# A long-convolution gate with a feed-forward branch: two equal column halves become 256 and 384, and the stages are ordered by half

## The chip, the cores and the metric

The kernel runs on one core of one Trainium2 chip. Five engines work side by side, each through its own queue in order: TensorE (PE in the profile, PEld for its weight loads), VectorE (DVE), ScalarE (ACT), GpSimd (POOL) and SyncE (SP). They wait for each other by semaphores. Transfers between the chip's memory (HBM) and the on-chip buffer (SBUF) are issued here by SP and POOL. Matmuls write to PSUM, and ScalarE or VectorE copies from there. The metric is the device time of one launch in microseconds (us).

## What is computed

`S` is 2048 positions, `D` 640 channels, `F` 1728. All inputs are bfloat16.

```python
x  = A_q
xn = _layernorm(x, axis=-1)
# A: short shift convolution, product, long convolution by FFT over 2*S
k_shift = sum(k_pad[:, t:t + S, :] * shift_k[:, ks - 1 - t] for t in range(ks))   # ks = 4
kv = k_shift * v
y  = irfft(rfft(kv padded to 2*S) * rfft(ssm_k padded to 2*S))[:S]
y  = y + kv * ssm_D
s  = xn * y
# B: feed-forward on the same xn
h  = gelu(xn @ w1 + b1)
g  = silu(h @ w2 + b2)
return x + s * g
```

## The kernel before

The Fourier transform over 2048 positions is done by matmuls, as a transform over 128 points and one over 16. Positions lie as 128 partitions by 16 columns of positions (`NT = 16`), and two of these columns (`n0`, `n0+1`) are one step. The 640 channels are cut into `DH = 2` halves of `DW = 320`, since two such blocks of float32 fit two PSUM banks of 512.

The work consists of generators; each `yield` ends a step:

- `early_loads` and `s_ln` (lines 142 and 188) load k, the filter and the constants, and make the normalised `XN_sb`.
- `s_hp` (219) transposes the filter `Hn` (`pt_h`, copied to `HTc` by ScalarE, all 640 channels at once), and calls `f1_pair` for both halves. `s_kv` (232) makes `KVc` on VectorE, one half after the other within each step, and calls `f1_pair` too.
- `f1_pair` (207) is the first transform: two PSUM tiles `ps_f`, copied by ScalarE to `A_sb` and written by POOL to a scratch tensor `ASC` in HBM.
- `s_mid(dh)` (301) takes one half: it loads `Z` from `ASC` (SP, two tiles for two pairs of rows each), makes the second transform of filter and signal (`ps_f2`, copied by ScalarE to `HFc` and `XFc`), multiplies on VectorE (`HSc`, `P1c`, `P2c`), transforms back (`ps_i`, lines 330 and 331), copies on VectorE to `Bc`, and writes that with POOL to a scratch tensor `BSC`. Each half has 16 such mid steps.
- `s_tail(dh)` (337) loads all of a half's `BSC` with one transfer to `BB`, and in eight steps makes the last transform (`ps_y`), multiplies with `XN_sb` (`sg`), adds x (`xin`, giving `ot`) and writes the output with POOL. It can only begin when the whole half has gone through `s_mid`, and each step needs the gate of its positions.
- `s_ffn` (260) is the feed-forward part in four quarters of 512 positions: transposes (`pt_x`), 70 matmuls with w1 (`ps_h`, 512 columns, to `HT` by ScalarE with gelu), then per 128 positions 14 matmuls with w2 for each half (`ps_o`, to `g_t` with silu), and a product that turns `XN_sb` into xn times g.

`run_plan` (362) interleaves these generators by start times and step times in a table (`PLAN_...`). From that text a scheduler makes each engine's order; it may put instructions earlier or later, so the order that counts is the one listed for the built program. Buffers set limits to it: the PSUM pool `pc` has two tiles for `ps_f`, `ps_i` and `ps_y` together, `pf` has four for the feed-forward part and the transposes.

## Time and profile before

| | |
|---|---|
| median of 3 timed runs | 308.36 us (308.19 to 311.12) |
| the profiled execution | 303.71 us |
| its span, first to last instruction | 301.9 us |
| mean granted TensorE clock in it | 0.945 of full |
| busy: TensorE, weight loads | 224.8 us (74%), 128.8 us (43%) |
| busy: VectorE, ScalarE, GpSimd | 183.1 us (61%), 169.6 us (56%), 78.6 us (26%) |
| moved between HBM and SBUF | 54.57 MB, 181 GB/s on the mean |

A row of a group names the line, the engine, the operation, what it writes and reads, and the shape, then how often it ran, its busy time in us and the mean of one in ns; behind the last bar stands how long the engine sat idle just before such instructions, and what ended that. A row of the timeline begins with the start and the duration in us; SPq is SP's queue, and there the duration includes waits. A row of the stretches gives for each engine the busy us and the count, then the granted clock, the share of time the DMA engines were busy, and GB/s. A row of the DMA issues gives the count, the size of one and the median us from issue to landing.

### The profile page before, as it was taken

Reading aid. Unit: us, or ns where it says so; the run is one execution under the profiler, and the core shown is the slowest. Engines: PE = TensorE matmul, PEld = TensorE weight load, DVE = VectorE, ACT = ScalarE, POOL = GpSimd, SP = SyncE. Lnnn points to the kernel's source line nnn. Section 1 sums busy time; section 2 is a strip of 40 time slices with the busy share of each in tenths; the row PEclk is TensorE's granted clock in tenths of the full one; section 3 lists DMA queues with packets and bytes.
Section 4 is the critical chain, followed back from the end, with each engine's and each line's share of the span. In section 5 each row is a group of like instructions: output and inputs, shape, how many; then the busy total and the mean of one; then the engine's idle time right before and its main releaser. Section 6 shows DMA issues by size and latency. Waiting matters only on the chain.

```text
span 301.9 us, 4066 instructions
## 1 busy us (share of the span) xinstructions
PE 224.8 (74%) x1360; PEld 128.8 (43%) x1360; DVE 183.1 (61%) x424; ACT 169.6 (56%) x267; POOL 78.6 (26%) x120
## 2 busy tenths in 40 slices
PE   3028147789799799979979999994999999920720
...
ACT  1248649999799459854548776450567655400000
...
PEclk9999999899999999999999999999799999985765
...
GB/s 165 265 337 278 358 402 353 166 199 140 167 130 187 229 121 97 129 230 111 130 130 139 146 130 134 109 234 289 132 170 138 114 168 176 66 157 255 114 190 43
DMA packets 33820, 54.57 MB, mean 181 GB/s; under 512 B 3268, under 2 KB 22790, under 8 KB 33672
## 3 DMA queue, kind: packets, MB, share of 16 engines
...
## 4 chain that ended last, share of the span: by engine, by line
issue 60%; POOL 18%; DMA 7%; DVE 5%; PE 3%; ACT 3%; SPq 1%; POOLq 1%; ACTq 0%; DVEq 0%
POOL ASC L217 9%; POOL BSC L334 6%; POOL out_dram L358 4%; DMA K_sb<-in_A_k_dram 3%; DMA Vc<-in_A_v_dram 3%; DVE stats L196 2%; DMA ASC<-A_sb 1%; PE ps_f L212 1%; ACT A_sb L216 1%; PE ps_o L293 1%; DVE tmp L250 1%; PE ps_h L281 1%; ACT XN_sb L204 1%; DVE acc L251 1%; DVE acc L244 0%
## 5 line engine op out<-in xcount | busy, mean ns | idle before, releaser
L281 PE MATMUL ps_h<-XT,W_sb 128*128 128x512 bf16 (+1 forms) x280 | 72.4, 388 | 1.6 <-ACT HT L284 1.6
L293 PE MATMUL ps_o<-W_sb,HT 128*128 128x320 bf16 x448 | 71.0, 299 | 0.1
L217 POOL DMA_DIRECT2D ASC<-A_sb x64 | 46.5, 728 | 77.4 <-ACT A_sb L216 77.0
L293 PEld LDWEIGHTS <-HT 128*128 128x128 bf16 x448 | 43.5, 97 | 18.8 <-issue 2.0
L216 ACT CAST A_sb<-ps_f 128x640 bf16<-128x640 f32 x64 | 41.8, 704 | 12.6 <-DMA ASC<-A_sb 8.7
L334 POOL DMA_DIRECT2D BSC<-Bc x32 | 17.7, 553 | 105.7 <-DVE Bc L333 105.7
L284 ACT ACTIVATE HT<-ps_h,B_sb 128x512 bf16<-128x512 f32 (+1 forms) x56 | 37.6, 699 | 6.2 <-PE ps_h L281 6.0
L281 PEld LDWEIGHTS <-W_sb 128*128 128x128 bf16 (+1 forms) x280 | 27.6, 100 | 31.2 <-issue 8.1
L333 DVE CAST Bc<-ps_i 128x640 bf16<-128x640 f32 x32 | 26.3, 823 | 17.5 <-PE ps_i L331 16.5
L318 ACT CAST HFc<-ps_f 128x640 bf16<-128x640 f32 x32 | 22.1, 691 | 25.7 <-PE ps_f L316 25.6
L316 PE MATMUL ps_f<-Z,SM 128*128 128x320 bf16 x128 | 29.4, 301 | 2.0 <-DMA Z<-ASC 1.6
L349 PE MATMUL ps_y<-BB,I2M 128*128 128x320 bf16 x64 | 14.7, 354 | 20.5 <-DMA BB<-BSC 17.0
L318 ACT CAST XFc<-ps_f 128x640 bf16<-128x640 f32 x32 | 22.2, 694 | 13.6 <-PE ps_f L316 8.8
L212 PEld LDWEIGHTS <-F1M 128*128 128x128 bf16 x128 | 12.9, 104 | 30.7 <-issue 15.9
L295 ACT ACTIVATE g_t<-ps_o 128x320 bf16<-128x320 f32 x32 | 14.0, 440 | 21.1 <-PE ps_o L293 21.1
L355 DVE TENSOR_TENSOR sg<-ps_y,XN_sb 128x640 bf16<-128x640 f32 x16 | 13.1, 820 | 17.8 <-PE ps_y L349 17.1
L212 PE MATMUL ps_f<-HTc,F1M 128*128 128x320 bf16 x64 | 16.8, 346 | 9.1 <-ACT A_sb L216 7.7
L296 DVE TENSOR_TENSOR XN_sb<-XN_sb,g_t 128x640 bf16<-128x640 bf16 x16 | 7.8, 489 | 24.3 <-ACT g_t L295 24.2
L330 PE MATMUL ps_i<-P1c,SM 128*128 128x320 bf16 x64 | 19.2, 300 | 4.1 <-DVE P1c L326 1.5
L326 DVE TENSOR_TENSOR P1c<-XFc,HFc 128x640 bf16<-128x640 bf16 x32 | 15.7, 492 | 10.6 <-ACT XFc L318 9.9
L212 PE MATMUL ps_f<-KVc,F1M 128*128 128x320 bf16 x64 | 14.4, 327 | 10.0 <-DVE KVc L253 7.2
L253 DVE TENSOR_TENSOR KVc<-acc,Vc 128x640 bf16<-128x640 bf16 x16 | 7.8, 489 | 21.4 <-PE ps_f L212 17.0
...
## 6 DMA issues: line engine op xcount, KB each, us to landing
ASC<-A_sb POOLq DMA_DIRECT2D x64, 160.0 KB, 2.9
Z<-ASC SPq DMA_DIRECT2D x32, 320.0 KB, 3.9
BSC<-Bc POOLq DMA_DIRECT2D x32, 160.0 KB, 2.6
BB<-BSC SPq DMA_DIRECT2D x2, 2560.0 KB, 13.1
Xc<-in_A_q_dram SPq DMA_DIRECT2D x8, 320.0 KB, 2.9
...
Vc<-in_A_v_dram SPq DMA_DIRECT2D x16, 160.0 KB, 3.0
```

What stands on the lines that cost most here:

```text
L212: nc.tensor.matmul(ps[:, j, 0:DW], lhsT=F1M[:, n0 + j, c, :], rhs=srcfn(j), start=True, stop=not fo)
L216: nc.scalar.copy(A_sb[:], ps[:, :, 0:DW])
L217: nc.gpsimd.dma_start(ASC[which, dh, c, n0:n0+2].rearrange("n k d -> k n d"), A_sb[:])
L281: nc.tensor.matmul(ps[0:fsz, :], lhsT=W1_sb[:, a, m*P:m*P+fsz], rhs=XT[:, a, :, :].rearrange("d n p -> d (n p)"), start=(a == 0), stop=(a ...
L284: nc.scalar.activation(HT[0:fsz, m, :], ps[0:fsz, :], ACT.Gelu_apprx_tanh, bias=B1_sb[0:fsz, m:m+1], scale=1.0)
L293: nc.tensor.matmul(ps[:, 0:DW], lhsT=HT[0:ksz, m, j*P:(j+1)*P], rhs=W2_sb[0:ksz, m, dh*DW:(dh+1)*DW], start=(m == 0), stop=(m == FT - 1))
L316: nc.tensor.matmul(ps[:, j, 0:DW], lhsT=SM[:, 0, :], rhs=Zt[which][:, kk + j, :], start=True, stop=True)
L318: nc.scalar.copy(dst[:], ps[:, :, 0:DW])
L326: nc.vector.tensor_tensor(out=P1c[:], in0=XFc[:], in1=HFc[:], op=ALU.mult)
L330: nc.tensor.matmul(ps[:, j, 0:DW], lhsT=SM[:, 1, :], rhs=P1c[:, j, :], start=True, stop=False)
L333: nc.vector.tensor_copy(Bc[:], ps[:, :, 0:DW])
L334: nc.gpsimd.dma_start(Bdst[:, k0:k0+2, :], Bc[:])
```

## The change

The halves become `DWS = (256, 384)`, that is two and three blocks of 128 channels. Everything that was indexed by equal halves goes by `DOFF` and `DWS`, tiles are allocated for the wider half, and each half has scratch tensors of its own. `s_hp` and `s_kv` now run through all positions of half 0 first and then through those of half 1; the filter's transposes and their copies are done for each half by itself. In `s_mid` every second `Bc` is copied by ScalarE instead of VectorE, and `HFc` and `XFc` have three buffers instead of two. `xin`, `sg` and `ot` share buffers with `Vc`, `acc` and `KVc`, three for the first and the last. The plan has shorter steps for `s_kv` and `s_hp` (there are twice as many), and earlier start times for the mid and tail parts.

```diff
+DWS = (256, 384)
+DOFF = (0, 256)
+DWM = 384
-PLAN_KV = 6.5
+PLAN_KV = 3.3
-PLAN_HP = 3.5
+PLAN_HP = 2.0
-PLAN_MID0 = 62.0
-PLAN_MID1 = 96.0
-PLAN_MIDSTEP = 2.1
-PLAN_TAIL0 = 100.0
-PLAN_TAIL1 = 134.0
+PLAN_MID0 = 40.0
+PLAN_MID1 = 80.0
+PLAN_MIDSTEP = 2.4
+PLAN_TAIL0 = 85.0
+PLAN_TAIL1 = 125.0
...
     for j in range(KS):
...
-        nc.vector.tensor_copy(W_bc[:, j, :].rearrange("p (h w) -> p h w", h=DH), ps[:, :, 0:DW])
+            nc.vector.tensor_copy(W_bc[:, j, DOFF[dh]:DOFF[dh]+DWS[dh]], ps[:, dh, 0:DWS[dh]])
...
-    ASC = tc.dram_tile([2, DH, 2, NT, P, DW], BF16, name="ASC")
-    BSC = tc.dram_tile([DH, P, 32, DW], BF16, name="BSC")
+    ASCs = [tc.dram_tile([2, 2, NT, P, DWS[dh]], BF16, name=f"ASC{dh}") for dh in range(DH)]
+    BSCs = [tc.dram_tile([P, 32, DWS[dh]], BF16, name=f"BSC{dh}") for dh in range(DH)]
...
     def s_hp():
...
-        for n0 in range(0, NT, 2):
-            HTc = hpp.tile([P, 2, D], BF16, name="HTc")
-            for j in range(2):
-                pt = pftile([P, DT, P], BF16, "pt_h")
-                for jj in range(DT):
-                    nc.tensor.transpose(pt[:, jj, :], Hn_v[:, jj, n0 + j, :], ident[:])
-                nc.scalar.copy(HTc[:, j, :].rearrange("p (a d) -> p a d", a=DT), pt[:])
-            for dh in range(DH):
-                f1_pair(1, lambda j, dh=dh: HTc[:, j, dh*DW:(dh+1)*DW], n0, dh, fold=True)
-            yield
+        for dh in range(DH):
+            tiles = (0, 1) if dh == 0 else (2, 3, 4)
+            for n0 in range(0, NT, 2):
+                HTc = hpp.tile([P, 2, DWM], BF16, name="HTc")
+                for j in range(2):
+                    pt = pftile([P, 3, P], BF16, "pt_h")
+                    for jj, a_ in enumerate(tiles):
+                        nc.tensor.transpose(pt[:, jj, :], Hn_v[:, a_, n0 + j, :], ident[:])
+                    nc.scalar.copy(HTc[:, j, 0:DWS[dh]].rearrange("p (a d) -> p a d", a=len(tiles)), pt[:, 0:len(tiles), :])
+                f1_pair(1, lambda j, HTc=HTc, dh=dh: HTc[:, j, 0:DWS[dh]], n0, dh, fold=True)
+                yield
...
     def s_kv():
-        for n0 in range(0, NT, 2):
-            for dh in range(DH):
-                dsl = slice(dh*DW, (dh+1)*DW)
-                Vc = kvp.tile([P, 2, DW], BF16, name="Vc")
+        for dh in range(DH):
+            DW = DWS[dh]
+            dsl = slice(DOFF[dh], DOFF[dh] + DW)
+            for n0 in range(0, NT, 2):
+                Vc = kvp.tile([P, 2, DWM], BF16, name="Vc", tag="Vc", bufs=3)
...
     def s_mid(dh):
...
-                Z = zc.tile([P, KG, DW], BF16, name=f"Z{which}", tag="z")
-                nc.sync.dma_start(Z[:], Zsrc[which][:, zi*KG:(zi+1)*KG, :])
+                Z = zc.tile([P, KG, DWM], BF16, name=f"Z{which}", tag="z")
+                nc.sync.dma_start(Z[:, :, 0:DW], Zsrc[which][:, zi*KG:(zi+1)*KG, :])
...
-                    dst = midp.tile([P, 2, DW], BF16, name="HFc" if which else "XFc")
-                    nc.scalar.copy(dst[:], ps[:, :, 0:DW])
+                    dst = midp.tile([P, 2, DWM], BF16, name="HFc" if which else "XFc", bufs=3)
+                    nc.scalar.copy(dst[:, :, 0:DW], ps[:, :, 0:DW])
...
-                nc.vector.tensor_copy(Bc[:], ps[:, :, 0:DW])
-                nc.gpsimd.dma_start(Bdst[:, k0:k0+2, :], Bc[:])
+                if (k0 // 2) % 2 == 0:
+                    nc.vector.tensor_copy(Bc[:, :, 0:DW], ps[:, :, 0:DW])
+                else:
+                    nc.scalar.copy(Bc[:, :, 0:DW], ps[:, :, 0:DW])
+                nc.gpsimd.dma_start(Bdst[:, k0:k0+2, :], Bc[:, :, 0:DW])
...
     def s_tail(dh, I2M):
...
-            xin = tlp.tile([P, 2, DW], BF16, name="xin")
-            nc.sync.dma_start(xin[:], xp[:, n0:n0+2, dh*DW:(dh+1)*DW])
+            xin = kvp.tile([P, 2, DWM], BF16, name="xin", tag="Vc", bufs=3)
+            nc.sync.dma_start(xin[:, :, 0:DW], xp[:, n0:n0+2, osl])
...
-            sg = tlp.tile([P, 2, DW], BF16, name="sg")
+            sg = kvp.tile([P, 2, DWM], BF16, name="sg", tag="acc")
...
-            ot = tlp.tile([P, 2, DW], BF16, name="ot")
+            ot = kvp.tile([P, 2, DWM], BF16, name="ot", tag="KVc", bufs=3)
```

Three places of the engines' orders show what moves. The first is ScalarE's queue at its end; the numbers are those of the tiles' copies. `HFc` and `XFc` are the casts of the last mid steps, `HT` the gelu and `g_t` the silu of the feed-forward part. Before:

```order
L318 CAST XFc_2817<-ps_f2_2814 128x640
L318 CAST HFc_2878<-ps_f2_2875 128x640
L295 ACTIVATE g_t_3000<-ps_o_3001 128x320
L318 CAST XFc_2883<-ps_f2_2880 128x640
L318 CAST HFc_2907<-ps_f2_2904 128x640
L318 CAST XFc_2912<-ps_f2_2909 128x640
L295 ACTIVATE g_t_3000<-ps_o_3017 128x320
L318 CAST HFc_2966<-ps_f2_2963 128x640
L318 CAST XFc_2971<-ps_f2_2968 128x640
L295 ACTIVATE g_t_3036<-ps_o_3037 128x320
L295 ACTIVATE g_t_3036<-ps_o_3053 128x320
```

After the change, the same end of ScalarE's queue (two more pairs of `g_t` stand behind these rows):

```order
L321 CAST XFc_2907<-ps_f2_2904 128x768
L286 ACTIVATE HT_162<-ps_h_2945,B1_sb_121 128x512
L339 CAST Bc_2921<-ps_i1_2916 128x768
L286 ACTIVATE HT_162<-ps_h_2952,B1_sb_121 128x512
L286 ACTIVATE HT_162<-ps_h_2959,B1_sb_121 64x512
L297 ACT_TABLE_LOAD
L297 ACTIVATE g_t_2966<-ps_o_2967 128x256
L297 ACTIVATE g_t_2966<-ps_o_2983 128x384
L297 ACTIVATE g_t_3014<-ps_o_3015 128x256
L297 ACTIVATE g_t_3014<-ps_o_3031 128x384
```

The last mid step now stands ahead of the end of quarter 3's w1 part and of all its w2 part; before, it stood in the last of that part's eight blocks. The last `Bc`, here on ScalarE, has an `HT` in front of it.

The second place is SP's queue where the first `Z` tiles are loaded. Before:

```order
L237 DMA Vc<-in_A_v_dram 128x2x320 x2
L345 DMA xin<-in_A_q_dram 128x2x320 x2
L237 DMA Vc<-in_A_v_dram 128x2x320 x9
L308 DMA Z_1488<-ASC 128x1280
L237 DMA Vc<-in_A_v_dram 128x2x320 x3
L384 DMA I2M<-I2M_d 128x4096
L308 DMA Z_1490<-ASC 128x1280
L308 DMA Z_1576<-ASC 128x1280
```

After the change, the same place:

```order
L243 DMA Vc<-in_A_v_dram 128x2x256 x7
L243 DMA Vc<-in_A_v_dram 128x2x384 x2
L311 DMA Z_1211<-ASC_165 128x4x256
L243 DMA Vc<-in_A_v_dram 128x2x384 x4
L311 DMA Z_1213<-ASC_165 128x4x256
L311 DMA Z_1362<-ASC_165 128x4x256
L311 DMA Z_1364<-ASC_165 128x4x256
L243 DMA Vc<-in_A_v_dram 128x2x384 x2
L311 DMA Z_1471<-ASC_165 128x4x256
L353 DMA xin<-in_A_q_dram 128x2x256
L311 DMA Z_1473<-ASC_165 128x4x256
```

The first two `Z` of the signal are now issued ahead of the last `Vc`, and three `xin`, which share buffers with `Vc`, stand between the following `Z`.

The third place is VectorE's queue behind its last mid step: `sg` and `ot` are steps of the tail, `XN_sb` the product with the gate. Before (`sg` and `ot` then go on in this way to the end):

```order
L333 CAST Bc_2985<-ps_i1_2980 128x640
L355 TENSOR_TENSOR sg_2995<-ps_y_2990,XN_sb_155 128x640
L357 TENSOR_TENSOR ot_2997<-sg_2995,xin_2988 128x640
L296 TENSOR_TENSOR XN_sb_155<-XN_sb_155,g_t_3036 128x640
L355 TENSOR_TENSOR sg_3077<-ps_y_3072,XN_sb_155 128x640
L357 TENSOR_TENSOR ot_3079<-sg_3077,xin_3070 128x640
L355 TENSOR_TENSOR sg_3089<-ps_y_3084,XN_sb_155 128x640
L355 TENSOR_TENSOR sg_3101<-ps_y_3096,XN_sb_155 128x640
L357 TENSOR_TENSOR ot_3091<-sg_3089,xin_3082 128x640
L355 TENSOR_TENSOR sg_3113<-ps_y_3108,XN_sb_155 128x640
```

After the change (six more steps, five of them of 768 columns, follow behind these):

```order
L298 TENSOR_TENSOR XN_sb_159<-XN_sb_159,g_t_2966 128x640
L298 TENSOR_TENSOR XN_sb_159<-XN_sb_159,g_t_3014 128x640
L298 TENSOR_TENSOR XN_sb_159<-XN_sb_159,g_t_3072 128x640
L363 TENSOR_TENSOR sg_3009<-ps_y_3004,XN_sb_159 128x768
L363 TENSOR_TENSOR sg_3055<-ps_y_3050,XN_sb_159 128x2x256
L365 TENSOR_TENSOR ot_3011<-sg_3009,xin_3002 128x768
L365 TENSOR_TENSOR ot_3057<-sg_3055,xin_3048 128x2x256
L363 TENSOR_TENSOR sg_3067<-ps_y_3062,XN_sb_159 128x768
L363 TENSOR_TENSOR sg_3113<-ps_y_3108,XN_sb_159 128x768
L365 TENSOR_TENSOR ot_3069<-sg_3067,xin_3060 128x768
L365 TENSOR_TENSOR ot_3115<-sg_3113,xin_3106 128x768
L298 TENSOR_TENSOR XN_sb_159<-XN_sb_159,g_t_3118 128x640
```

Ten tail steps now stand behind the last mid step, eight of them of the wide half, with four gate products ahead of or among them; before there were ten as well, of 320 channels, and one product.

88 lines of the change are left out of this document (44 added, 44 removed).

## Prediction

> **What bounds the kernel now.** I read the page's forty slices first, then the stretches of the span, then the waits, then the last 40 us of the timeline.
>
> ```profile
> PE   3028147789799799979979999994999999920720
> ...
> ACT  1248649999799459854548776450567655400000
> ...
> PEclk9999999899999999999999999999799999985765
> ```
>
> Each digit is the busy share of one slice of 7.5 us. TensorE is nearly full from the eleventh slice to the thirty-fifth; it is poorly filled in the first eight and in the last five, where the granted clock falls too. ScalarE is full only around 50 to 75 us. The stretches below are cut at my own places: loading, quarter 0 of the feed-forward part, the w1 half of quarter 1, the rest up to the last spectral product, the wait for the last big load, the end.
>
> ```profile
> core 0: us, PE busy (x) PEld busy (x) DVE busy (x) ACT busy (x) POOL busy (x), PEclk, DMA share, GB/s
> 0.00:47.60 47.60, 16.89 (x88) 8.52 (x89) 35.57 (x108) 24.23 (x37) 9.68 (x18) 1.00 0.87 305
> 47.60:107.50 59.90, 51.93 (x324) 30.54 (x323) 35.21 (x85) 50.80 (x82) 30.95 (x43) 0.97 0.59 184
> 107.50:128.30 20.80, 20.30 (x116) 10.20 (x115) 8.04 (x19) 17.33 (x27) 8.70 (x12) 1.00 0.41 126
> 128.30:264.50 136.20, 126.08 (x793) 74.72 (x793) 90.21 (x190) 76.85 (x121) 21.46 (x37) 0.99 0.49 152
> 264.50:281.00 16.50, 3.52 (x19) 1.91 (x18) 3.30 (x6) 0.44 (x1) 1.25 (x2) 0.64 0.68 189
> 281.00:301.90 20.90, 6.11 (x29) 2.92 (x27) 10.78 (x17) 0.00 (x0) 6.54 (x9) 0.66 0.43 125
> ```
>
> From 107.5 to 264.5 us TensorE is busy 146 of 157 us: there the order of work hardly matters and the amount of TensorE work does. From 264.5 on nothing is left for it but the inverse transform of half 1, which has to wait:
>
> ```profile
> PEld L349 <- DMA BB<-BSC: 17.5, 2, 13.3
> ...
> DVE Bc L333 <- PE ps_i L331: 16.5, 26, 0.7
> ...
> DVE P1c L326 <- ACT XFc L318: 9.9, 20, 1.3
> ...
> ACT A_sb L216 <- DMA ASC<-A_sb: 8.7, 5, 3.6
> ```
>
> The columns are microseconds in total, times, and the longest. The first row is two waits, 13.3 us and 4.2 us: the loads of BB for half 1 and half 0. The timeline shows both.
>
> ```profile
> 205.83 1.28 PE L274 MATMUL pt_x<-ident,XN_sb 128*128 128x128 bf16 x20
> 211.09 1.25 PE L349 MATMUL ps_y<-BB,I2M 128*128 128x320 bf16 x4 [3.98 <-DMA BB<-BSC]
> ...
> 264.19 0.30 PE L331 MATMUL ps_i<-P2c,SM 128*128 128x320 bf16 x1
> ...
> 264.60 1.25 PE L293 MATMUL ps_o<-W_sb,HT 128*128 128x320 bf16 x8
> ...
> 265.64 0.54 POOL L334 DMA_DIRECT2D BSC<-Bc  x1 [2.61 <-DVE Bc L333]
> ...
> 267.91 0.37 SPq L339 DMA_DIRECT2D BB<-BSC  x1
> ...
> 278.83 5.00 PE L349 MATMUL ps_y<-BB,I2M 128*128 128x320 bf16 x20 [12.98 <-DMA BB<-BSC]
> 280.11 0.82 DVE L355 TENSOR_TENSOR sg<-ps_y,XN_sb 128x640 bf16<-128x640 f32 x1 [13.11 <-PE ps_y L349]
> ...
> 294.75 0.49 DVE L357 TENSOR_TENSOR ot<-sg,xin 128x640 bf16<-128x640 bf16 x1 [1.07 <-DMA out_dram<-ot]
> ```
>
> The last ps_i ends at 264.5; its Bc is written out, BB is issued at 267.9, TensorE goes on at 278.8, VectorE works the last nine steps off until 295.2, and the span ends 6.7 us later. So 37.4 us lie behind the last ps_i, with eight ps_o the only feed-forward work among them. That tail is what this change can shorten.
>
> **The change, part by part.** Prices first: two runs without a gap, then the groups.
>
> ```profile
> 101.30 6.29 PE L293 MATMUL ps_o<-W_sb,HT 128*128 128x320 bf16 x45
> ...
> 115.96 5.56 PE L281 MATMUL ps_h<-XT,W_sb 128*128 128x512 bf16 x25
> ```
>
> ```profile
> L216 ACT CAST A_sb<-ps_f 128x640 bf16<-128x640 f32 x64 | 41.8, 704 | 12.6 <-DMA ASC<-A_sb 8.7 <-PE ps_f L212 2.7 <-ACT A_sb L216 0.9
> L227 ACT COPY HTc<-pt_h 128x640 bf16<-128x640 bf16 x16 | 10.8, 701 | 0.0
> L284 ACT ACTIVATE HT<-ps_h,B_sb 128x512 bf16<-128x512 f32 (+1 forms) x56 | 37.6, 699 | 6.2 <-PE ps_h L281 6.0
> L284 ACT ACT_TABLE_LOAD x5 | 6.4, 1283 | 0.1
> L295 ACT ACTIVATE g_t<-ps_o 128x320 bf16<-128x320 f32 x32 | 14.0, 440 | 21.1 <-PE ps_o L293 21.1
> L333 DVE CAST Bc<-ps_i 128x640 bf16<-128x640 f32 x32 | 26.3, 823 | 17.5 <-PE ps_i L331 16.5 <-DMA BSC<-Bc 0.9
> L355 DVE TENSOR_TENSOR sg<-ps_y,XN_sb 128x640 bf16<-128x640 f32 x16 | 13.1, 820 | 17.8 <-PE ps_y L349 17.1
> L357 DVE TENSOR_TENSOR ot<-sg,xin 128x640 bf16<-128x640 bf16 x16 | 7.9, 491 | 3.1 <-DMA out_dram<-ot 2.7
> ```
>
> A streamed matmul takes 1.28/20 = 0.064 us at 128 columns, 0.140 at 320, 0.222 at 512. That is a straight line, so I read 0.115 at 256 and 0.167 at 384, together 0.282 against 2 x 0.140: the uneven halves cost TensorE nothing. ScalarE takes 0.440 us for 320 columns and 0.704 for 640, so 0.18 fixed and 0.000825 a column: 0.60 for 512, 0.81 for 768. VectorE's PSUM reads are known at one size only; for 768 columns between 0.82 and 0.98 I take 0.97, for 512 between 0.66 and 0.82 I take 0.66 (in proportion, since no row shows a fixed part); ot likewise 0.58 and 0.39.
>
> *Feed-forward work goes behind the last ps_i.* Counted in the two orders of TensorE's instructions, the old one has 440 of 448 ps_o, all 280 ps_h and 26 ps_y ahead of the last ps_i; the new one has 336, 274 and 24. That is 104 x 0.140 + 6 x 0.222 + 2 x 0.140 = 16.2 us less, and 24 narrower ps_y save 24 x 0.025 = 0.6. Since TensorE bounds that stretch: -16.8 us.
>
> *Transposes of the filter by halves.* The 16 HTc copies become 32 and the transposes stay 80: 16 x 0.18 = +2.9 us of ScalarE, in a stretch where it is busy 50.8 of 59.9 us. A 6.3 us run of 45 ps_o there shows that it has some slack. Between 0 and 2.9 I take +2. Eight W_bc copies in place of four fall in the first 11 us, where the loads are awaited: nothing, unless those become short.
>
> *The mid part of half 0 beside the rest of kv.* Seven mid steps and ten A_sb now lie beside the 70 ps_h of quarter 1. TensorE: 15.5 + 28 x 0.115 + 24 x 0.115 + 20 x 0.167 + 1.3 for XT = 26.1 us. ScalarE: 14 HT 9.8, a table load 1.3, 14 casts 8.4, some 3.5 Bc 2.1, ten A_sb 8.1: 29.7 us. ScalarE becomes the bound there, by 3.6 us; the same 3.6 would partly have gone into the small waits of the mid steps (rows above: at most 1.3 us each). I take +2, ends 0 and 6. They all share the two PSUM buffers of pc.
>
> *Mid steps: wider for half 1, every other Bc on ScalarE, three HFc/XFc.* VectorE loses 16 x 0.82 = 13 us, ScalarE gains 16 x 0.70 = 11; neither bounds this stretch on the average (90 and 77 of 136 us). Casts of half 1 are 0.11 us longer each and those of half 0 0.10 shorter. In sum I take +1, near nothing since each part is small and has work beside it; the ends are -5 and +12, worked out as rivals (c) and (b).
>
> *BB of half 0.* Its load waits for the last BSC of half 0 and stands in SP's queue behind four Z loads, with 20% fewer bytes than before.
>
> ```profile
> ASC<-A_sb POOLq DMA_DIRECT2D x64, 160.0 KB, 2.9
> Z<-ASC SPq DMA_DIRECT2D x32, 320.0 KB, 3.9
> BSC<-Bc POOLq DMA_DIRECT2D x32, 160.0 KB, 2.6
> BB<-BSC SPq DMA_DIRECT2D x2, 2560.0 KB, 13.1
> ```
>
> 4.3 us to its issue and 10.5 to 13.1 to land make 15 to 17; between them TensorE has 36 ps_h, 8.0 us, and three mid steps, 21 matmuls of 384 columns, 3.5, with 0.5 of waiting each: 13. It waits 2 to 4 us, as before 4.0: nothing. The Z tiles of half 0 become rows of 512 bytes; they are loaded a group of two mid steps ahead, some 6 us (2.61 + 0.54 from one BSC issue to the next at 265.64), against 3.9 to land. Were the landing twice as long for four times as many rows, 7.8, some 1.5 us would be missing in each of eight groups; I take nothing, as the bytes fall by a fifth. xin shares buffers with Vc and so waits on SP for a KVc, with Z loads queued behind; on VectorE those KVc stand ahead of the mid steps that need these Z: nothing.
>
> So the last ps_i ends at 264.5 - 16.8 + 2 + 2 + 1 = 252.7. *Behind it:* Bc is now a ScalarE copy with an HT in front of it, so BB is issued 3.4 + 0.9 = 4.3 us later. 3072 KB land in between 10.9 us (278.8 - 267.9, if bytes don't count) and 13.1 x 1.2 = 15.7; I take 14.4, since 13.1 is the nearest row and part of it grows. TensorE meanwhile has six ps_h, 51 ps_o of 256 and 42 of 384 columns, 1.3 + 5.9 + 7.0 = 14.2 us, so it waits about 4.5 us at 271.4, not 13. From there VectorE sets the pace: 8 x 1.55 + 2 x 1.05 + 0.5 = 15.0 us, 0.7 for the first ps_y, 0.5 of gaps, 6.7 to the end: 22.9. The last 19 ps_o lie beside it. The end is 252.7 + 4.3 + 14.4 + 22.9 = 294.3, **7.6 us under the 301.9 of this span**.
>
> The profiled execution took 303.71 us, 4.65 under the median of 308.36, so I carry the difference over: 308.36 - 7.6 = **300.8 us**.
>
> Two rules of the Trainium skill bear on the tail. "DMA: Bandwidth & Descriptors", Specifications, has transfers run at line rate from 512 bytes on; by that BB's time goes with its bytes, 15.7 us, and the sum would be 302.1. "TensorE: Matmul & The Clock Gate", Part 1, halves the clock after about 3.4 us of idling; the row at 211.09 agrees, four ps_y in 1.25 us after a wait of 3.98. A wait of 4.5 us with 19 ps_o behind it would then cost up to 19 x 0.15 = 2.9 us, an estimate, and the sum would be 303.7 if VectorE did not cover it.
>
> **The rivals.** *(a) Given back in ScalarE's queue.* Quarter 3's ps_h run beside seven steps of half 1: ScalarE 9.8 + 1.3 + 7 x 2.03 = 25.3 us, TensorE 15.5 + 9.4 + 1.9 = 26.8. Two queues this equal, each in order, wait for each other; a fifth more there and in quarters 1 and 2 is 5 to 6 us, and with BB at 15.7 the gain falls to about 1: 307. For it: XFc already keeps P1c waiting 9.9 us. Against: ScalarE was busy only 77 of 136 us.
>
> *(b) Slower: Bc behind HT.* The ps_i buffer is free only when Bc is copied, and the next XFc matmul wants it. On ScalarE Bc stands behind an HT or g_t (0.70) and partly HFc (0.81). If TensorE stands still for that in 16 steps at 0.75 us, 12 us are added: 308.36 - 7.6 + 12 = 312.8. It decides for slower from (7.6 + 3.1)/16 = 0.67 us a step. Against: two to fourteen feed-forward matmuls stand between.
>
> *(c) Much faster.* Three HFc/XFc buffers and the freer VectorE remove the small waits in the mid steps: from 107.5 to 264.5 TensorE lacks 10.6 us, 4.0 of them the wait for BB of half 0, so some 5 more are to be had: with BB at 10.9 the time is 300.8 - 5 - 3.5 = 292.3.
>
> **How the numbers follow.** My forecast (a gain of 4 to 11 us) gets 0.5, (a) 0.2, (b) 0.17, (c) 0.13. A per cent, 3.1 us, is about what a measurement of this kernel can tell from no change. Faster by more than that: the forecast and (c), 0.63; within: (a), 0.2; slower: (b), 0.17. The range goes from 293, just inside (c), to 311, inside (b); outside lie some 0.07 below and 0.12 above. The forecast's own range is 297 to 305.
>
> **What would show it.** Right: the last ps_i near 253 us, some 112 ps_o behind it, one wait of 3 to 6 us for BB of half 1, and VectorE without gaps for the last 15 us. Wrong: a last ps_i behind 258 (ScalarE or Bc: then ps_f waits for Bc or A_sb), BB of half 1 landing later than 16 us after its issue, or quarter 0 ending later than 111 us.

## The result, and the profile after

The changed kernel takes 289.92 us (median of 12 runs, 288.06 to 294.36), the kernel before beside it 307.01 (15 runs, 304.14 to 311.12). The ratio is 0.9452, with a 95% interval of 0.9418 to 0.9486: faster by 5.5%, where 2.5% was forecast. The ratios here compare only executions in the faster of two states that the runs show, so they can differ a little from the quotient of the medians. The time lies below the range that was given. The profiled execution of the changed kernel took 290.16 us, its span 288.4.

The busy tenths in forty slices of the changed kernel (7.2 us each):

```profile
PE   4062047699989876999999889799998899997830
...
ACT  1267554999898756988865487757462888721000
...
PEclk9998555799999999999999999999999999998895
```

TensorE now is nearly full until the last two slices, and the granted clock reads 8, 8, 9, 5 tenths in the last four where it read 5, 7, 6, 5. It is low in the loading phase instead (slices five to eight), where TensorE is busy 0 to 7 tenths of the time.

The same stretches as before the change, cut at the same places of the work, but for the last cut, which here is the first ps_y of half 1 and in the prediction's rows stands 2.2 us behind it (TensorE, its weight loads, VectorE, ScalarE, GpSimd busy, then granted clock, DMA share and GB/s):

```profile
0.00:44.80 44.80, 13.07 (x80) 7.52 (x81) 28.63 (x96) 21.68 (x38) 8.74 (x16) 0.79 0.83 287
44.80:106.80 62.00, 54.69 (x333) 31.69 (x334) 42.62 (x102) 52.70 (x95) 30.35 (x42) 0.93 0.62 197
106.80:137.70 30.90, 26.66 (x158) 14.20 (x157) 19.07 (x46) 25.22 (x41) 12.11 (x17) 1.00 0.52 162
137.70:248.10 110.40, 103.08 (x636) 59.56 (x634) 65.84 (x145) 72.44 (x114) 22.23 (x35) 1.00 0.51 163
248.10:264.00 15.90, 13.90 (x100) 9.49 (x99) 1.48 (x3) 5.96 (x10) 0.54 (x1) 1.00 0.71 212
264.00:288.40 24.40, 11.38 (x59) 6.35 (x59) 13.48 (x21) 0.87 (x2) 7.23 (x10) 0.80 0.40 129
```

In the fifth row TensorE waits for the last BB: it is busy 13.9 of 15.9 us there, before the change 1.35 of the 14.3 us up to that ps_y.

The waits of the changed kernel (total us, times, longest):

```profile
ACT A_sb L220 <- DMA ASC<-A_sb: 11.5, 10, 2.8
DVE Bc L337 <- PE ps_i L334: 11.4, 15, 2.4
...
DVE P1c L329 <- ACT XFc L321: 4.7, 9, 0.8
PEld L357 <- DMA BB<-BSC: 4.5, 2, 2.3
...
PE ps_y L357 <- DMA BB<-BSC: 3.5, 2, 2.0
...
DVE ot L365 <- DMA out_dram<-ot: 1.1, 1, 1.1
```

TensorE's two waits for BB fell from 17.0 us (3.98 and 12.98) to 3.5, P1c's wait for XFc from 9.9 to 4.7. The timeline of the changed kernel from the last ps_i on (start, duration, engine, line, operation; in brackets the idle time before and what ended it):

```profile
247.73 0.32 PE L334 MATMUL ps_i<-P2c,SM 128*128 128x384 bf16 x1
...
249.40 12.60 PE L295 MATMUL ps_o<-W_sb,HT 128*128 128x256 bf16 x93
...
251.57 0.37 SPq L347 DMA_DIRECT2D BB<-BSC  x1
...
264.00 1.40 PE L357 MATMUL ps_y<-BB,I2M 128*128 128x384 bf16 x8 [2.00 <-DMA BB<-BSC]
264.86 1.55 DVE L363 TENSOR_TENSOR sg<-ps_y,XN_sb 128x768 bf16<-128x768 f32 x2 [2.79 <-PE ps_y L357]
...
278.19 0.56 DVE L365 TENSOR_TENSOR ot<-sg,xin 128x768 bf16<-128x768 bf16 x1 [1.06 <-DMA out_dram<-ot]
...
280.40 1.02 DVE L365 TENSOR_TENSOR ot<-sg,xin 128x768 bf16<-128x768 bf16 x2
```

One run of 93 ps_o covers the load of BB almost wholly. Against the forecast, stretch by stretch, on the two profiled executions:

| stretch | before | after | change | forecast |
|---|---|---|---|---|
| start to the first ps_h | 47.6 | 44.8 | -2.8 | 0 |
| quarter 0: first ps_h to its last ps_o | 60.0 | 62.0 | +2.0 | +2 |
| from there to the end of the last ps_i | 156.9 | 141.3 | -15.6 | -13.8 |
| last ps_i to the first ps_y of half 1 | 14.3 | 15.9 | +1.6 | +4.4 |
| from there to the end | 23.1 | 24.4 | +1.3 | -0.2 |
| span | 301.9 | 288.4 | -13.5 | -7.6 |

### The profile page after: what moved, and what is told of

It reads as the page before. It is cut to its first block, busy times and chain, and to the rows that moved or that the text cites. A ratio compares the mean times of both kernels' runs of the same rounds, so it can differ in the third digit from the quotient of the medians.

```text
span 288.4 us, 4094 instructions
## 1 busy us (share of the span) xinstructions
PE 222.8 (77%) x1360; PEld 128.8 (45%) x1360; DVE 171.1 (59%) x412; ACT 178.9 (62%) x299; POOL 81.2 (28%) x120
## 3 DMA queue, kind: packets, MB, share of 16 engines
q0 software_dynamic: 6272, 18.36, 18.7%
## 4 chain that ended last, share of the span: by engine, by line
issue 50%; POOL 19%; DMA 10%; ACT 7%; PE 7%; DVE 5%; POOLq 1%; SPq 0%; ACTq 0%; DVEq 0%
POOL ASC L221 10%; POOL BSC L340 6%; DMA ASC<-A_sb 4%; POOL out_dram L366 4%; DMA K_sb<-in_A_k_dram 3%; PE ps_h L283 3%; DMA Xc<-in_A_q_dram 2%; ACT XN_sb L207 2%; PE ps_f L216 2%; ACT A_sb L220 2%; DVE stats L199 2%; ACT L286 1%; DVE acc L253 1%; PE pt_x L276 1%; PE ps_f L319 0%
## 5 line engine op out<-in xcount | busy, mean ns | idle before, releaser
L295 PE MATMUL ps_o<-W_sb,HT 128*128 128x256 bf16 (+1 forms) x448 | 71.3, 301 | 0.2 <-ACT HT L286 0.2
L220 ACT CAST A_sb<-ps_f 128x512 bf16<-128x512 f32 (+1 forms) x64 | 43.2, 712 | 17.7 <-DMA ASC<-A_sb 11.5
L283 PEld LDWEIGHTS <-W_sb 128*128 128x128 bf16 (+1 forms) x280 | 27.7, 101 | 33.9 <-issue 11.1
L319 PE MATMUL ps_f<-Z,SM 128*128 128x256 bf16 (+1 forms) x128 | 27.8, 298 | 3.7 <-ACT A_sb L220 2.3
L321 ACT CAST HFc<-ps_f 128x512 bf16<-128x512 f32 (+1 forms) x32 | 22.3, 697 | 11.9 <-PE ps_f L319 11.4
L216 PE MATMUL ps_f<-KVc,F1M 128*128 128x256 bf16 (+1 forms) x64 | 14.5, 307 | 17.0 <-DVE KVc L255 14.7
L321 ACT CAST XFc<-ps_f 128x512 bf16<-128x512 f32 (+1 forms) x32 | 22.5, 703 | 2.9 <-PE ps_f L319 1.6
L253 DVE TENSOR_TENSOR acc<-acc,tmp 128x512 bf16<-128x512 bf16 (+1 forms) x48 | 23.2, 485 | 0.5
L333 PE MATMUL ps_i<-P1c,SM 128*128 128x256 bf16 (+1 forms) x64 | 19.1, 298 | 4.8 <-DVE P1c L329 3.7
L252 DVE TENSOR_TENSOR tmp<-K_sb,W_bc 128x512 bf16<-128x512 bf16 (+1 forms) x48 | 21.9, 481 | 0.1
L216 PE MATMUL ps_f<-HTc,F1M 128*128 128x256 bf16 (+1 forms) x64 | 15.2, 331 | 5.7 <-ACT HTc L233 3.1
```

The lines of the kernel that those rows point to most:

```text
L216: nc.tensor.matmul(ps[:, j, 0:DW], lhsT=F1M[:, n0 + j, c, :], rhs=srcfn(j), start=True, stop=not fo)
L220: nc.scalar.copy(A_sb[:, :, 0:DW], ps[:, :, 0:DW])
L252: nc.vector.tensor_tensor(out=tmp[:, :, 0:DW], in0=src, in1=wb, op=ALU.mult)
L253: nc.vector.tensor_tensor(out=acc[:, :, 0:DW], in0=acc[:, :, 0:DW], in1=tmp[:, :, 0:DW], op=ALU.add)
L283: nc.tensor.matmul(ps[0:fsz, :], lhsT=W1_sb[:, a, m*P:m*P+fsz], rhs=XT[:, a, :, :].rearrange("d n p -> d (n p)"), start=(a == 0), stop=(a ...
L295: nc.tensor.matmul(ps[:, 0:DWS[dh]], lhsT=HT[0:ksz, m, j*P:(j+1)*P], rhs=W2_sb[0:ksz, m, DOFF[dh]:DOFF[dh]+DWS[dh]], start=(m == 0), stop= ...
```

## The experiments

Five theories were set against each other. A: the gain is feed-forward work put behind the last ps_i. B: it is relief in the mid steps (a third buffer, Bc on ScalarE, a narrow first half). C, formed after the second group of runs: the third buffers work in the tail, where `ot` and `xin` take turns in the tags KVc and Vc. D and E are about the tail of two later variants. Runs that stand under one heading shared a chip and the runs of the kernel before.

### The plan, the widths and Bc, one at a time

*The kernel before once more*, unchanged.

> The kernel before once more, for a second profile. All theories: ratio 1.00 within half a per cent. The first profile of it took 303.71 us where its timed runs have a median of 307; if that execution was simply a quick one, this span is some 2 to 4 us longer than 301.9, spread over the span. If the difference lies in one place, that place shows what the change may have removed unseen.

308.6 us, ratio 1.0013 (0.9952 to 1.0074). So a single comparison is good to about half a per cent at best; the repeats of the changed kernel below lie up to 0.9% apart. The span of this second profile is 308.0 us, 6.1 more than the first, where 2 to 4 more were expected, and it is spread out: 0.5 us up to the first ps_h, 2.0 in quarter 0 at a granted clock of 0.94 instead of 0.97, 3.1 from there to the last ps_i, 0.6 in the wait for BB of half 1.

*The changed kernel with the old plan:*

```diff
-PLAN_KV = 3.3
+PLAN_KV = 3.25
-PLAN_HP = 2.0
+PLAN_HP = 1.75
-PLAN_MID0 = 40.0
-PLAN_MID1 = 80.0
-PLAN_MIDSTEP = 2.4
-PLAN_TAIL0 = 85.0
-PLAN_TAIL1 = 125.0
+PLAN_MID0 = 62.0
+PLAN_MID1 = 96.0
+PLAN_MIDSTEP = 2.1
+PLAN_TAIL0 = 100.0
+PLAN_TAIL1 = 134.0
```

> The changed kernel with the start and step times of the plan before for the mid and tail parts (s_kv and s_hp keep their pace, at half the old step). Halves of 256 and 384, order by half, Bc on two engines and three buffers stay. Behind the last ps_i stand 18 ps_o instead of 112. Theory A (the feed-forward work that covers the load of BB and the wide tail is the gain): most of the gain goes, ratio 0.985 to 1.00, and TensorE waits 11 us or more for BB of half 1. Theory B (relief in the mid steps by buffers, by Bc on ScalarE and by the narrow half): at least half of the gain stays, ratio 0.97 or lower.

303.59 us, ratio 0.986 (0.9764 to 0.9956): of 5.5% gain 1.4 are left. Its timeline:

```profile
260.42 2.88 PE L295 MATMUL ps_o<-W_sb,HT 128*128 128x256 bf16 x18
...
264.46 0.37 SPq L347 DMA_DIRECT2D BB<-BSC  x1
...
276.54 2.31 PE L357 MATMUL ps_y<-BB,I2M 128*128 128x384 bf16 x8 [13.24 <-DMA BB<-BSC]
```

Only 18 ps_o stand behind the last ps_i, and the wait of 13 us is back. Widths, buffers and Bc are those of the changed kernel, so they explain little by themselves. Theory A holds for the larger part. What is left fits the wait for BB of half 0, which stays as short as in the changed kernel (1.49 us, with a granted clock of 1.00 behind it, against 3.98 and 0.58 before); with the width of this interval that is not shown.

*Equal halves in the new order:*

```diff
-DWS = (256, 384)
-DOFF = (0, 256)
-DWM = 384
+DWS = (320, 320)
+DOFF = (0, 320)
+DWM = 320
...
-            tiles = (0, 1) if dh == 0 else (2, 3, 4)
+            tiles = (0, 1, 2) if dh == 0 else (2, 3, 4)
+            h0 = 0 if dh == 0 else 64
...
-                f1_pair(1, lambda j, HTc=HTc, dh=dh: HTc[:, j, 0:DWS[dh]], n0, dh, fold=True)
+                f1_pair(1, lambda j, HTc=HTc, dh=dh, h0=h0: HTc[:, j, h0:h0+DWS[dh]], n0, dh, fold=True)
```

> The changed kernel with halves of 320 and 320; the middle block of 128 channels of the filter is transposed twice, 16 transposes (1 us of TensorE) and 16 x 0.13 us of ScalarE more. Theory A: as the change, ratio 0.940 to 0.955, since the tail then has 20 per cent fewer columns behind BB. If the uneven split itself is worth something (half 0 sooner, less for the first mid steps): 0.96 or higher.

293.91 us, ratio 0.9555 (0.9459 to 0.9651), just above the 0.940 to 0.955 that A gave.

*Bc on VectorE alone:*

```diff
-                if (k0 // 2) % 2 == 0:
-                    nc.vector.tensor_copy(Bc[:, :, 0:DW], ps[:, :, 0:DW])
-                else:
-                    nc.scalar.copy(Bc[:, :, 0:DW], ps[:, :, 0:DW])
+                nc.vector.tensor_copy(Bc[:, :, 0:DW], ps[:, :, 0:DW])
```

> The changed kernel with every Bc on VectorE again. Theory A: 0.940 to 0.950, no difference that counts. Theory B: VectorE is fuller by 13 us in the mid steps and each ps_i buffer is held longer, ratio 0.96 or higher. My own fear in the prediction (a Bc in ScalarE's queue holds the PSUM buffer) would make this kernel faster than the change, 0.935 or lower.

294.53 us, ratio 0.9585 (0.9487 to 0.9683), between what A and B gave. Both ratios lie 1.1 and 1.4% above the changed kernel's; the interval of the equal halves overlaps with its interval, that of Bc on VectorE begins where its interval ends, and a later repeat of the changed kernel gave 0.9539. What is certain is that neither carries the gain. The stretch from quarter 0 to the last ps_i is 139.9 us with equal halves and 141.3 with Bc on VectorE, against 141.3, but in both some ps_h moved out of it, behind the last ps_i: 14 (3.1 us) and 10 (2.2 us). So with Bc on VectorE the mid part is some 2 us worse for the same work, and its trace says where: ps_i waits 8.3 us in 15 waits for P1c of VectorE, in the changed kernel 3.7 us in 9.

```profile
PE ps_i L333 <- DVE P1c L329: 8.3, 15, 2.0
```

So theory B has a share here, of a size that these runs can only just tell.

### Buffers, a dense plan before, the wide half first, an earlier plan

*Two buffers instead of three:*

```diff
-                Vc = kvp.tile([P, 2, DWM], BF16, name="Vc", tag="Vc", bufs=3)
+                Vc = kvp.tile([P, 2, DWM], BF16, name="Vc", tag="Vc", bufs=2)
...
-                KVc = kvp.tile([P, 2, DWM], BF16, name="KVc", tag="KVc", bufs=3)
+                KVc = kvp.tile([P, 2, DWM], BF16, name="KVc", tag="KVc", bufs=2)
...
-                    dst = midp.tile([P, 2, DWM], BF16, name="HFc" if which else "XFc", bufs=3)
+                    dst = midp.tile([P, 2, DWM], BF16, name="HFc" if which else "XFc")
```

`xin` and `ot` in the tail, which use the tags Vc and KVc, get two as well.

> The changed kernel with two buffers each for HFc/XFc, Vc and KVc, as before the change, instead of three; widths, order and the copies on ScalarE stay. The work behind the last ps_i is that of the changed kernel (6 ps_h, 112 ps_o). Theory A (the gain is feed-forward work put behind the last ps_i): within 1% of the changed kernel, a ratio to the kernel before of 0.935 to 0.955. Theory B (the gain is relief in the mid steps: buffers, ScalarE, a narrow first half): ScalarE and VectorE wait for each other once per step, the stretch from the end of quarter 0 to the last ps_i grows from 141.6 us by 3 to 6, ratio 0.955 to 0.965.

296.26 us, ratio 0.9596 (0.9559 to 0.9633): the time that B gave, but not in the place that B gave. The stretch to the last ps_i is 141.4 us, as with three buffers. From the first ps_y of half 1 to the issue of the last store it is 21.6 us instead of 18.7, and VectorE's `ot` waits 5.2 us for output stores, instead of 1.1. From this came theory C.

*The kernel before with a denser mid part:*

```diff
-PLAN_MID0 = 62.0
-PLAN_MID1 = 96.0
-PLAN_MIDSTEP = 2.1
-PLAN_TAIL0 = 100.0
-PLAN_TAIL1 = 134.0
+PLAN_MID0 = 61.0
+PLAN_MID1 = 88.0
+PLAN_MIDSTEP = 1.6
+PLAN_TAIL0 = 91.0
+PLAN_TAIL1 = 118.0
```

> The kernel before with equal halves, its old order of loops and its two buffers; only five plan numbers differ, so that the mid steps of half 1 stand closer together: the first matmul of the mid part stands where it stood, but 62 ps_o instead of 8 stand behind the last ps_i. Theory A: 54 x 0.14 = 7.6 us of ps_o go into TensorE's wait of 13 us for BB; last ps_i some 7 us earlier, the wait about 5.5 us, ratio 0.970 to 0.980 to the kernel before. Theory B: without a narrower first half, a third buffer and copies on ScalarE the denser mid steps of the old kernel are held up by VectorE; the last ps_i comes less than 3 us earlier, ratio 0.99 or more.

301.29 us, ratio 0.9726 (0.9672 to 0.978), as A gave it: half of the whole gain from five numbers in the plan, with nothing else of the change. The stretch from quarter 0 to the last ps_i is 147.9 us, 9.0 less than in the first profile of the kernel before. Not all of it is the 54 ps_o (7.6 us by the price above): the wait for BB of half 0 fell here too, from 3.98 us to 1.44, with a clock of 1.00 behind it. The timeline shows the 62 ps_o and what is left of the wait for half 1:

```profile
261.64 8.60 PE L293 MATMUL ps_o<-W_sb,HT 128*128 128x320 bf16 x62
265.22 0.37 SPq L339 DMA_DIRECT2D BB<-BSC  x1
276.01 5.01 PE L349 MATMUL ps_y<-BB,I2M 128*128 128x320 bf16 x20 [5.76 <-DMA BB<-BSC]
```

*The wide half first:*

```diff
-DWS = (256, 384)
-DOFF = (0, 256)
+DWS = (384, 256)
+DOFF = (0, 384)
-            tiles = (0, 1) if dh == 0 else (2, 3, 4)
+            tiles = (0, 1, 2) if dh == 0 else (3, 4)
```

> The changed kernel with the wide half first (384, then 256), everything else as it is. 21 ps_h and 112 ps_o stand behind the last ps_i. Theory A: what is behind the last ps_i decides, and it is as much as before or more; BB of half 1 is 2048 KB instead of 3072 and lands about 2 us sooner, the last eight steps of VectorE are narrower (684+420 instead of 952+551 ns, 8 x 0.4 = 3.2 us), against that the wide BB of half 0 makes TensorE wait 2 to 3 us longer in the middle and quarter 0 about 1 us longer: ratio 0.930 to 0.945, no slower than the changed kernel. Theory B: the narrow first half is what lets the mid part begin early; ratio 0.955 or more, with quarter 0 or the waits of ScalarE in the first mid part longer by 3 us and more.

300.07 us, ratio 0.9738 (0.9687 to 0.9789): A's forecast failed, and B's time and its longer quarter 0 came. In the profile (296.18 us, the fastest of its runs) quarter 0 takes 67.2 us, against 62.0 to 63.7 in the three profiles of the changed kernel (up to 66.4 in its variants) and 64.6 with equal halves. But the end is as much longer: from the first ps_y of half 1 on it takes 29.3 us instead of 24.4, though its steps are narrower.

```profile
255.03 6.26 PE L295 MATMUL ps_o<-W_sb,HT 128*128 128x384 bf16 x42
265.07 1.04 PE L357 MATMUL ps_y<-BB,I2M 128*128 128x256 bf16 x4 [3.78 <-DMA BB<-BSC]
```

Only 42 of the 112 ps_o, with 21 ps_h, stand ahead of that ps_y and cover the load, which leaves a wait of 3.78 us; the other 70 come among the ps_y. The profiled execution alone doesn't account for the whole of the median's loss.

*An earlier plan:*

```diff
-PLAN_MID0 = 40.0
-PLAN_MID1 = 80.0
-PLAN_MIDSTEP = 2.4
-PLAN_TAIL0 = 85.0
-PLAN_TAIL1 = 125.0
+PLAN_MID0 = 36.0
+PLAN_MID1 = 74.0
+PLAN_MIDSTEP = 2.3
+PLAN_TAIL0 = 79.0
+PLAN_TAIL1 = 117.0
```

> The changed kernel with five plan numbers made smaller, so that the mid part stands earlier and denser: 48 ps_h instead of 6 stand behind the last ps_i (42 x 0.222 = 9.3 us more). Theory A: only the 2.0 us that TensorE still waits for BB can be covered; the last ps_i comes 7 to 9 us earlier, BB lands while TensorE still has work, and the rest of the moved work lies on the path behind it: ratio 0.937 to 0.947, a gain of at most 2 us on the changed kernel. Theory B: fewer feed-forward matmuls beside the mid steps leave TensorE waiting for VectorE and ScalarE; the last ps_i comes less than 4 us earlier and the time is 3 us or more above the changed kernel, ratio 0.955 or more.

289.68 us, ratio 0.9385 (0.9343 to 0.9426). The last ps_i comes 4.2 us earlier than in the changed kernel, less than the 7 to 9 that A gave (the stretch from quarter 0 on is 7.4 us shorter, quarter 0 itself 2.8 longer in this execution), and the end of the span at the same time. Its timeline on TensorE:

```profile
243.68 10.64 PE L283 MATMUL ps_h<-XT,W_sb 128*128 128x512 bf16 x47
254.25 3.82 PE L295 MATMUL ps_o<-W_sb,HT 128*128 128x256 bf16 x27
259.48 1.47 PE L357 MATMUL ps_y<-BB,I2M 128*128 128x384 bf16 x8 [1.41 <-DMA BB<-BSC]
...
262.00 3.65 PE L295 MATMUL ps_o<-W_sb,HT 128*128 128x256 bf16 x25
```

The ps_h take the place of ps_o under BB's load, and the ps_o move behind it, in among the ps_y. Once the wait is covered, more work behind the last ps_i only lengthens the tail. The interval overlaps that of the changed kernel and lies below that of its slowest repeat, so a gain on it of up to 1% is neither shown nor excluded.

The same count orders the other runs. Of the 112 ps_o behind the last ps_i, 93 stand ahead of half 1's first ps_y in the changed kernel and 19 among the ps_y; with Bc on VectorE it is 79 and 33, with equal halves 59 and 53, with the wide half first 42 and 70, here 27 and 85. From that ps_y to the end these profiles take 24.4, 25.8, 27.0, 29.3 and 28.8 us. So A's count of what stands behind the last ps_i was too coarse: only what stands ahead of the first ps_y covers the load. This is read off the traces; no run changes that split alone.

### Which third buffer

*The changed kernel again, as a yardstick.*

> The changed kernel once more, as the yardstick for the three runs beside it. In the first profile quarter 0 took 62.0 us, the stretch from there to the last ps_i 141.3, the stretch behind the last ps_i 34.7 (to the end of the last output store's issue). Expected: ratio to the kernel before 0.938 to 0.950; the stretch to the last ps_i within 1 us of 141.3; quarter 0 anywhere from 62 to 65 us, as in the other kernels with the same order there. A ratio of 0.955 or more would mean that the cost seen with two buffers was the chip's and not the buffers'.

293.14 us, ratio 0.9539 (0.9483 to 0.9595): above the 0.938 to 0.950 that was expected, just below the 0.955 that would have put the cost of two buffers down to the chip. The stretch to the last ps_i is 140.2 us. The two runs below that differ in their buffers alone are better told from each other than from this yardstick.

*Two buffers for HFc and XFc alone:*

```diff
-                    dst = midp.tile([P, 2, DWM], BF16, name="HFc" if which else "XFc", bufs=3)
+                    dst = midp.tile([P, 2, DWM], BF16, name="HFc" if which else "XFc")
```

> The changed kernel with two buffers for HFc and XFc alone; Vc and KVc keep three. Theory C (the third buffers work in the tail, since ot and xin share the tags KVc and Vc): within 0.7% of the unchanged changed kernel beside it, the stretch from the end of quarter 0 to the last ps_i 141 to 142 us as in the run with two buffers everywhere (141.4), VectorE's wait of ot for output stores near 1 us. Theory B (the third buffer relieves the mid steps): 1.0 to 1.8% slower than the run beside it, by a longer stretch to the last ps_i.

290.92 us, ratio 0.944 (0.9386 to 0.9493). No loss, and even 0.8% below the yardstick's median, where C gave at most 0.7% either way; the stretch to the last ps_i is 140.9 us. The third buffer of HFc and XFc does nothing that these runs show.

*Two buffers for Vc and KVc, and so for `xin` and `ot`:*

```diff
-                Vc = kvp.tile([P, 2, DWM], BF16, name="Vc", tag="Vc", bufs=3)
+                Vc = kvp.tile([P, 2, DWM], BF16, name="Vc", tag="Vc", bufs=2)
...
-                KVc = kvp.tile([P, 2, DWM], BF16, name="KVc", tag="KVc", bufs=3)
+                KVc = kvp.tile([P, 2, DWM], BF16, name="KVc", tag="KVc", bufs=2)
```

> The changed kernel with two buffers for Vc and KVc, and with them for xin and ot; HFc and XFc keep three. Theory C: the whole cost of the run with two buffers everywhere: 1.0 to 1.8% slower than the changed kernel beside it, VectorE's ot waits some 5 us for output stores in the tail instead of 1.1, and the stretch from quarter 0 to the last ps_i stays at 141 to 142 us. Theory B: within 0.7% of the changed kernel.

296.71 us, ratio 0.963 (0.9584 to 0.9675): 1.2% above the yardstick's median and 2.0% above the run with two HFc. VectorE's waits from 255 us on, with two buffers for `ot`:

```profile
DVE ot L365 <- DMA out_dram<-ot: 5.0, 5, 1.8
```

and with three, in the last repeat of the changed kernel (below):

```profile
DVE ot L365 <- DMA out_dram<-ot: 1.8, 2, 1.0
```

Theory C holds: the stretch from the first ps_y of half 1 to the last store's issue is 21.6 and 21.5 us in the two profiles with two buffers, 18.7, 18.6, 18.0 and 18.0 in the three of the changed kernel and the one with two HFc. Against the yardstick alone the 1.2% would not be clear, as the two intervals overlap; against the run with two HFc, and for all buffers against the first run of the changed kernel, they do not. With two buffers the last `sg` and `ot` also stand in VectorE's queue by turns, one and one, so their order moved a little with the buffers.

*Four buffers for KVc, and so for `ot`, two for HFc and XFc:*

```diff
-                    dst = midp.tile([P, 2, DWM], BF16, name="HFc" if which else "XFc", bufs=3)
+                    dst = midp.tile([P, 2, DWM], BF16, name="HFc" if which else "XFc")
...
-                KVc = kvp.tile([P, 2, DWM], BF16, name="KVc", tag="KVc", bufs=3)
+                KVc = kvp.tile([P, 2, DWM], BF16, name="KVc", tag="KVc", bufs=4)
...
-            ot = kvp.tile([P, 2, DWM], BF16, name="ot", tag="KVc", bufs=3)
+            ot = kvp.tile([P, 2, DWM], BF16, name="ot", tag="KVc", bufs=4)
```

> The changed kernel with two buffers for HFc and XFc and four for KVc, that is for ot: memory moved from the mid steps to the tail. Theory C: the 1.1 us that ot still waits for output stores goes, nothing is lost in the middle: 0 to 0.6% faster than the changed kernel beside it. Theory B: 1% or more slower than the changed kernel.

291.35 us, ratio 0.9456 (0.9405 to 0.9507): no faster than the run with two HFc and three KVc. The waits for stores are gone and that stretch is 16.1 us, 1.9 to 2.6 less; but quarter 0 takes 66.4 us.

### The tail once more

*`ot` by turns from the three buffers of KVc and the two of tmp*, which moves no instruction:

```diff
-            ot = kvp.tile([P, 2, DWM], BF16, name="ot", tag="KVc", bufs=3)
+            ot = kvp.tile([P, 2, DWM], BF16, name="ot", tag="KVc" if n0 % 4 == 0 else "tmp", bufs=3 if n0 % 4 == 0 else 2)
```

> The changed kernel with ot taken by turns from KVc's three buffers and tmp's two; no instruction moves on any engine (with four KVc buffers the filter products of kv moved forward in VectorE's queue in quarter 0). Theory D (the run with four buffers gained its 2.5 us in the tail and gave them back in quarter 0, 66.4 us, by kv work pulled forward): the tail from the first ps_y of half 1 to the last store's issue is 16 to 17 us instead of 18.6, quarter 0 stays at 62 to 64 us, and the time is 0.5 to 1.0% below the changed kernel beside it. Theory E (the quarter's length was the execution's, and the end is not set by ot): no more than 0.3% from the changed kernel.

291.4 us, ratio 0.944 (0.9365 to 0.9516), and beside it *the changed kernel a third time*:

> The changed kernel, as the yardstick on this chip: ratio 0.940 to 0.957; quarter 0 62 to 64 us, tail from the first ps_y of half 1 18.0 to 18.7 us.

290.79 us, ratio 0.9463 (0.941 to 0.9516). So a fourth and fifth buffer for `ot` gain nothing that can be measured. The profile can't tell D from E by its stretches: in that execution BB of half 1 landed late (a wait of 4.2 us), the clock fell to 0.50 behind it, and the stretch to the last store's issue is 19.0 us. Whether four KVc lengthen quarter 0 stays open.

*The earlier plan with `ot` from two tags:*

> The denser mid plan (48 ps_h behind the last ps_i) together with ot by turns from two tags. In the denser plan ot hardly waited for stores (0.3 us), TensorE's ps_o set the tail. Theory D: no gain on the denser plan alone, 0.935 to 0.945 to the kernel before, 0 to 1% below the yardstick. If the two gains added up it would be 1.5% or more below the yardstick.

289.67 us, ratio 0.9422 (0.936 to 0.9484), within the yardstick's interval. The gains don't add up, and no variant is shown to be faster than the changed kernel.

## Why the prediction was right in kind and half in size

The forecast of 300.8 is 10.9 us above what was measured. 5.9 of them are the span (294.3 forecast, 288.4 measured); 4.9 are the step from the span to the median. By the table of stretches the 5.9 are 2.8 at the start, 1.8 up to the last ps_i and 2.8 in the wait behind it, less 1.5 lost in the tail.

**The step "I carry the difference over"** failed. The profiled execution of the kernel before stood 4.65 us under its median, that of the changed kernel 0.24 above. The execution of before was quicker than every timed run of it (304.0 to 312.9 us over all groups), so the sum on it was compared with an unusually good before. The difference belonged to that execution and not to the kernel's work, and adding it to the other kernel had no ground. The second profile of before, 6.1 us longer, shows a lower granted clock in its longer stretches; why before's executions spread so far wasn't settled.

**"Feed-forward work goes behind the last ps_i": -16.8.** Right in kind, shown from both sides: with the old plan three quarters of the gain go, and in the kernel before five plan numbers, which put 54 more ps_o behind the last ps_i and shortened the wait of the next point, give 2.7%. TensorE's busy time from quarter 0 to the last ps_i fell by 16.6 us (146.4 to 129.7), of which 1.6 are the next point; that leaves 15.0 for the moved work.

**"BB of half 0 ... as before 4.0: nothing"** failed as a term put at nothing. With 2048 KB instead of 2560, half 0's load took 10.2 us from its issue to TensorE's next matmul instead of 13.1, and the wait fell from 3.98 us to 1.55. More than that: the windows behind the wait, in the kernel before, the changed one and the one with equal halves, show the clock in the third column from the right:

```profile
211.10:215.00 3.90, 3.90 (x14) 1.90 (x15) 1.96 (x4) 0.78 (x2) 0.72 (x1) 0.58 0.26 67
```

```profile
187.50:191.50 4.00, 3.92 (x21) 2.01 (x22) 2.47 (x5) 1.92 (x3) 1.23 (x2) 1.00 0.57 195
```

```profile
195.70:200.00 4.30, 4.30 (x25) 2.26 (x26) 2.85 (x6) 2.66 (x4) 0.71 (x1) 1.00 0.38 97
```

Behind the idle 3.98 us the granted clock was 0.58 for 3.9 us, which costs some 3.9 x 0.42 = 1.6 us, an estimate; behind 1.55 us, and behind 2.8 in the kernel with equal halves, it was 1.00. So 2.4 + 1.6 = 4.0 us came from a place that was put at nothing. The Trainium skill, "TensorE: Matmul & The Clock Gate", Part 1, throttles after an idle window of about 3.4 us. These three rows agree, as does the second profile of the kernel before (0.50 for 4.2 us behind a wait of 4.64); the prediction had applied that rule to the tail and not here. In the tail of the changed kernel it doesn't hold as a limit for a single wait: behind only 2.00 us of waiting the clock was 0.63.

```profile
264.00:267.90 3.90, 3.90 (x19) 2.40 (x20) 2.35 (x4) 0.38 (x1) 0.73 (x2) 0.63 0.00 0
```

In the kernel with equal halves the wait for half 1, 2.75 us, was followed by 0.57, the one for half 0, 2.78 us, by 1.00. So waits of 2 to 3 us went either way, and the length of the wait alone doesn't tell which.

**"The mid part of half 0 beside the rest of kv": +2.** 3.7 us were measured: in the w1 part of quarter 1 TensorE is idle 4.2 of 30.9 us (third row of the windows), before 0.5 of 20.8. TensorE's 26.1 us there were 26.7, but ScalarE is busy 25.2, not 29.7: the stretch is longer than either, by TensorE's waits for A_sb of ScalarE (2.9 us) and for P1c of VectorE (1.1). **"Mid steps": +1.** Nothing to be seen: idle time elsewhere up to the last ps_i fell by 0.4 us. The two-sided end of -5 to +12 was far too wide: the third buffers of HFc and XFc moved that stretch by less than 1 us, and Bc on ScalarE is worth some 2 us in it for the same work. The waits of rival (a) came in quarter 1, as the 3.7 us say, and nowhere else to be seen; of rival (b), 0.8 us in one wait of ps_f for Bc. (c), which came nearest to the time, had the wrong cause in the middle, where its three buffers do nothing and TensorE's idle time grew from 10.5 to 11.6 us; its other half, an early BB, came in part.

**"Transposes of the filter by halves": +2** came out as a number, 62.0 us against 60.0, but not shown as a cause. The granted clock in quarter 0 was 0.93 against 0.97, the second profile of the kernel before took 62.0 us there too, at 0.94, and the repeats of the changed kernel took 62.7 and 63.7. The groups of the changed kernel by shape, next to the prices that the prediction took:

```profile
L337 DVE CAST Bc<-ps_i 128x768 bf16<-128x768 f32 x8 | 7.7, 957 | 7.3 <-PE ps_i L334 7.3
...
L363 DVE TENSOR_TENSOR sg<-ps_y,XN_sb 128x768 bf16<-128x768 f32 x8 | 7.4, 952 | 3.7 <-PE ps_y L357 3.7
L233 ACT COPY HTc<-pt_h 128x384 bf16<-128x384 bf16 x16 | 6.9, 520 | 0.0
...
L339 ACT CAST Bc<-ps_i 128x768 bf16<-128x768 f32 x8 | 6.4, 799 | 7.6 <-issue 3.9 <-PE ps_i L334 3.1 <-ACT HT L286 0.7
```

0.97 and 0.81 had been taken for VectorE and ScalarE at 768 columns.

**What no term held: the start.** The first ps_h comes 2.8 us earlier; in all thirteen other profiles of kernels with the new order of loops the first one recorded comes at 44.7 to 46.8 us, 0.9 to 3.0 before the 47.6 of the kernel before. In the kernel before it stands behind the filter's ps_f, which wait for A_sb, whose buffers wait for their stores (3.6 us in one wait):

```profile
44.94 0.69 PE L212 MATMUL ps_f<-HTc,F1M 128*128 128x320 bf16 x2 [3.86 <-ACT A_sb L216]
47.15 0.69 PE L212 MATMUL ps_f<-HTc,F1M 128*128 128x320 bf16 x2 [1.52 <-ACT A_sb L216]
47.63 2.34 PE L281 MATMUL ps_h<-XT,W_sb 128*128 128x512 bf16 x5
```

In the changed kernel it waits for its own weights:

```profile
44.78 4.45 PE L283 MATMUL ps_h<-XT,W_sb 128*128 128x512 bf16 x10 [1.25 <-DMA W_sb<-in_B_w_dram]
```

The order of the loops changed there too, and the prediction began its sum at the first ps_h. That the order is what moved it was not tested by itself.

**Behind the last ps_i.** BB was issued 3.5 us after it, not 4.3, and TensorE went on 12.4 us after the issue, not 14.4. The row of 13.1 us that the prediction leant on times half 0's load alone, in the middle of the kernel; half 1's load before took 10.9 us, and 20% more bytes took 1.5 us more. With 3072 KB at this place it took 11.9 to 12.4 us in ten of twelve profiles, 13.4 and 14.6 in the other two. The Trainium skill, "DMA: Bandwidth & Descriptors", Specifications, has line rate from transfers of 512 bytes on, and the prediction read that as time in proportion to the bytes, 15.7 us. The proportion is not borne out here; a fixed part with some 350 GB/s behind it (an estimate: 512 KB more in 1.5 us) would fit these two loads as well. The tail then took 24.4 us instead of 22.9: VectorE, forecast with 0.5 us of gaps, needs 16.6 us from the first sg to the last ot instead of 15.5, with gaps for ps_y (behind the low clock) and for a free `ot`. The third buffer of `ot` was not priced at all; without it 3 more would have been lost, 1.2 to 2% of the time.
